# Keeping the upsampled rows out of x: logits per group and a second gather

## The chip, the cores and the metric

The kernel runs on one core of one Trainium2 chip. The metric is the device time of one launch in microseconds; the number shown for the kernel before is the median of three runs. The engines are TensorE (PE, with its weight loads PEld), VectorE (DVE), ScalarE (ACT), GpSimd (POOL) and SyncE (SP), whose queue issues most transfers.

## The reference

Two stages are computed: an attention with a downsampled and a local part, and a layer of eight experts over its result. Cut to what matters:

```python
def _attn_ref(q, k, v):                       # 8 batches, 8 heads, 576 tokens, 64 dims
    q_d, k_d, v_d = [z.reshape(B, H, 144, 4, D).mean(axis=3) for z in (q, k, v)]
    out_up = np.repeat(sm_attn(q_d, k_d, v_d), 4, axis=2)
    mask = np.abs(pos[:, None] - pos[None, :]) < 4
    out_local = masked softmax attention of q, k, v
    return out_up + out_local

def _moe_ref(x, w_gate, w1, w2):              # x: 4608 tokens x 512
    logits = x @ w_gate                       # 8 experts, 576 tokens each
    order = np.argsort(-logits.flatten())
    # in this order a token goes to an expert while the token is free and the expert has room
    for e in range(8):
        out[assigned == e] = np.maximum(x[assigned == e] @ w1[e], 0) @ w2[e]
```

`out_up` has one row for four tokens: 1152 different rows of 512 numbers, against 4608 rows of x. The logits are linear in x.

## The kernel before

**Attention** (class Attention) works on 36 units of 128 tokens, four and a half units to a batch. For each batch q, k and v are loaded and transposed, the downsampled attention is computed (`down`), and its rows are written from the tile `xu` to `up_dram` in DRAM (L387, L394). For each unit `loc_s`, `loc_t` and `loc_v` compute the local attention into the tile `x`. `load_up` (L416) loads the unit's 32 rows of `up_dram`, each into four partitions (256 KB). `log_a` (L484) adds them into x, on DVE for the first 28 units and on POOL after that. `store` (L487) writes x to `x_dram`. `log_t` transposes x on PE (L494) and writes it as two float16 parts with ACT (L498) and DVE (L499). `log_m` multiplies them by the gate weights (L509, L512) and sums into the logits `lg` (L514).

The order of this stage is written by hand. `run` gives each piece of work a time in units, `at`, sorts by it and issues the work in that order on every queue. The times of a unit's steps are its number plus the lags of this table:

```python
LOC = {'up': 1.7, 'st': 4.6, 't': 1.3, 'lm': 8.07, 's0': 0.33, 's1': 0.331, 'lt': 5.61, 'v0': 1.83, 'v1': 1.831, 'add': 4.5}
UPQ = STQ = "sync"
```

`end[b]` is the time at which the downsampled attention of batch b is done; no up load stands ahead of it. Loads of q, k and v, the stores and the loads of up rows all go through SP's queue, in this order.

**Routing** (class Routing) finds for each expert the tokens that it gets: DVE compares the logits' codes with thresholds (L703), PE counts (L733, L744), and the chain ends in the token numbers `idx` (L1004). `ro.phase` does it for one expert; that of the next expert runs beside the present one.

**Experts** (class Experts). `gather` fetches an expert's 576 rows of `x_dram` in five indirect transfers on POOL (L1068), of 128 rows each and of 64 the last. For experts 0 and 1 `piece` transposes each part on PE (L1077), with ACT and DVE writing the two float16 parts `xt` (L1080, L1081). For later experts ACT and DVE first write the parts as `xs` (L1087, L1088), and SP's queue transposes them by a transfer (L1089). `mlp` computes the hidden layer in eight slices f of 128 (L1104; for each slice 24 matmuls into `pH`, then ACT and DVE write `ht`, L1117 and L1120), then five chunks of output rows (L1133, `pX`), their eviction (L1139) and their scatter on POOL (L1142). The next expert's weights are split into float16 parts beside it (L1051 on ACT, L1053 on DVE). In expert 0 the table

```python
GET0 = {3: (0, 1), 4: (2, 3, 4)}
```

sets expert 1's pieces: 0 and 1 are transposed after the matmuls of chunk 3, ahead of chunk 4, the rest after chunk 4. From here on the framework's scheduler sets the order, by priorities and by when it takes operands to be ready.

Of the kernel before, what the change touches and what calls it, by code (L numbers as in the profile page):

```python
# [49 lines left out]
LOC = {'up': 1.7, 'st': 4.6, 't': 1.3, 'lm': 8.07, 's0': 0.33, 's1': 0.331, 'lt': 5.61, 'v0': 1.83, 'v1': 1.831, 'add': 4.5}  # L50
# [3 lines left out]
UPQ = STQ = "sync"  # L54
NSW = 2
UB = 3
XB = 6
# [3 lines left out]
ADDU = 28  # L61
DX = 0
SETUP = {25:0,35:26}
# [26 lines left out]
class Attention:  # L90
    def __init__(self, ctx, tc, q, k, v, wg, ident, identb, maskc, x_dram, up_dram, lg, big, more=()):
        self.tc, self.nc = tc, tc.nc
        self.q, self.k, self.v = q, k, v
        self.x_dram, self.up_dram, self.lg = x_dram, up_dram, lg
# [22 lines left out]
        self.vw, self.vd, self.qz, self.qdz, self.qdt, self.sw, self.ptw = [], [], [], [], [], [], []  # L117
        self.sd = cst.tile([128, 9, G], F32, name="sd")
# [291 lines left out]
    def load_up(self, u):  # L410
        for b in {4 * u // NW, (4 * u + 3) // NW}:
            for g in range(2):
                self.need(("v", b, g))
        t = self.wk.tile([128, HD], F32, name="up", bufs=UB)
        src = self.up_dram[32 * u:32 * u + 32]
        getattr(self.nc, UPQ).dma_start(t, bass.AP(tensor=src.tensor, offset=src.offset, ap=[[HD, 32], [0, 4], [1, HD]]))  # L416
        self.up[u] = t

# [59 lines left out]
    def log_a(self, u):  # L481
        nc = self.nc
        x = self.x[u]
        (nc.gpsimd if u >= ADDU else nc.vector).tensor_tensor(x, x, self.up[u], op=OP.add)  # L484

# [3 lines left out]
    def log_t(self, u):  # L489
        nc = self.nc  # L490
        x = self.x[u]
        p = self.ps.tile([128, 4, 128], F32, name="g", bufs=8)
        for c in range(4):
            nc.tensor.transpose(p[:, c], x[:, 128 * c:128 * c + 128], self.ident)  # L494
        xt = self.wk.tile([128, 2, 4, 128], F16, name="xt", bufs=TB)
# [4 lines left out]
                                                              op0=OP.mult, op1=OP.subtract), ("x", u))  # L500
        self.xt[u] = xt

    def log_m(self, u):
        nc = self.nc
        self.need(("x", u))
        xt = self.xt.pop(u)
# [7 lines left out]
        nc.vector.tensor_reduce(self.lg[:, u], l.rearrange("p s e -> p e s"), axis=AX.X, op=OP.add)  # L514
# [23 lines left out]
    def run(self, after, ready):  # L538
# [14 lines left out]
        for b in range(B):  # L553
# [27 lines left out]
            "up": lambda u: lambda: self.load_up(u),  # L581
            "st": lambda u: lambda: self.store(u),
            "add": lambda u: lambda: self.log_a(u),
# [5 lines left out]
        for u in range(NT):  # L589
            if u > 1:  # L590
                work.append((u - VWT, 0, 0, lambda u=u: self.load_vw(u), False))
            for j, (name, lag) in enumerate(LOC.items()):
                at = u + lag
                if lag >= 2.0:

                    at += max(E0 - u * E1, 0.0) - max(u - UE, 0) * CE * int(lag - 1)
                if name == "up":
                    at = max(at, end[(4 * u + 3) // NW])
                work.append((at, 2, j, stage[name](u), name in PEL))
                if name == "lm" and u in SETUP:  # L600
                    steps = after(SETUP[u], u + 1)
                    work += [(at + SPACE * k, 3, k, lambda g=steps: next(g, None), False) for k in range(24)]
# [405 lines left out]
class Experts:  # L1008
    def __init__(self, ctx, tc, x_dram, w1, w2, out, ident, ps, raw):
        self.tc, self.nc, self.x, self.w1, self.w2, self.out, self.ps = tc, tc.nc, x_dram, w1, w2, out, ps  # L1010
        self.raw = raw
# [47 lines left out]
    def gather(self, idx, first):  # L1059


        nc = self.nc
        xt = self.wk.tile([128, 2, 4, CAP], F16, name="xt")
        xgs = []
        for c, (s0, n) in enumerate(SL):
            xg = self.wk.tile([128, HD], F32, name="xg", bufs=5)
            with self.tc.high_priority():
                self.fetched = nc.gpsimd.indirect_dma_start(out=xg[:n], out_offset=None, in_=self.x,  # L1068
                                                            in_offset=bass.IndirectOffsetOnAxis(
                                                                ap=idx[:n, c:c + 1], axis=0))  # L1070
            xgs.append(xg)
# [22 lines left out]
    def mlp(self, w, xt, idx, in1, in2):  # L1094
# [4 lines left out]
        for f in range(8):  # L1099
            p = self.ps.tile([128, 2, 512], F32, name="pH", bufs=2)  # L1100
            seq = [(d, a, b) for d in range(4) for a, b in ((0, 0), (0, 1), (1, 0))]
            for s, (s0, s1) in enumerate(CUT):
                for j, (d, a, b) in enumerate(seq):
                    mm = nc.tensor.matmul(p[:, s, :s1 - s0], w[d][a][:, 128 * f:128 * f + 128], xt[:, b, d, s0:s1],  # L1104
                                          start=j == 0, stop=j == len(seq) - 1)
            if f == AFT:
                aft = mm
            with self.tc.high_priority():
                los = []
                for i, (n0, n1) in enumerate(((0, 256), (256, 320))):  # L1110
                    q = p[:, :, n0:n1] if i == 0 else p[:, 1:, n0:n1]
                    m = q.shape[1]
                    s0 = 0 if i == 0 else 512
                    hi = ht[:, f, s0:s0 + m * (n1 - n0)].rearrange("p (s n) -> p s n", s=m)
                    o0 = CAP + 64 if i == 0 else CAP
                    lo = ht[:, f, o0:o0 + m * (n1 - n0)].rearrange("p (s n) -> p s n", s=m)
# [4 lines left out]
            in1(f, last)  # L1121
# [27 lines left out]

FREE = 0  # L1150
# [8 lines left out]
def moe_attention(tc, q, k, v, wg, w1, w2, cst, out):  # L1159
    nc = tc.nc  # L1160
    with ExitStack() as top:
# [3 lines left out]
        up_dram = dr.tile([B * G, HD], F32, name="up_dram")  # L1165
        lg = keep.tile([128, NT, E], F32, name="lg")
# [121 lines left out]
```

## Time and profile before

| | us |
|---|---|
| median of three runs (798.14 to 803.59) | 799.38 |
| the profiled execution | 802.95 |
| its span on the core | 801.2 |
| PE busy | 684.2 (85%) |
| DVE busy | 563.2 (70%) |
| ACT busy | 331.7 (41%) |
| POOL busy | 249.4 (31%) |

The mean granted clock of TensorE is 0.929 of full speed. The numbers in the next sections come from this one execution. A line of its timeline gives start, length, engine, line of the kernel, operation, tiles and count, and in brackets how long the engine was idle before it and what ended that. The attention ends at about 299 us, when the last logits are reduced; the routing of the first expert takes until 327 us, when its first gather starts; the experts take the rest.

### The profile page before, as it was taken

The numbers are of one execution on the slowest core, as the hardware profiler recorded it, in microseconds if no ns is written. First come the engines' busy times: TensorE is split into PE (matmuls) and PEld (weight loads), VectorE is DVE, ScalarE is ACT, GpSimd is POOL, SyncE is SP. The second block draws the span as 40 slices with busy tenths as digits, with TensorE's granted clock in tenths as the row PEclk, the third lists the DMA queues.
The fourth block names the chain that finished last, engine by engine and source line by source line (L and its number), as shares of the span: only waits on it lengthen the run. The fifth ranks groups of instructions, "written<-read, shape, count | busy, mean of one in ns | idle before, by whom it ended". The sixth has DMA issues, their size and how long they took to land. (4 is left out here: it accounts for less than half of the span.)

```text
span 801.2 us, 21182 instructions
## 1 busy us (share of the span) xinstructions
PE 684.2 (85%) x8565; PEld 470.8 (59%) x8565; DVE 563.2 (70%) x1679; ACT 331.7 (41%) x631; POOL 249.4 (31%) x274
## 2 busy tenths in 40 slices
PE   6587978895998863499899899999989979999994
PEld 4576867774787752365465365475456456574752
DVE  7787977986797887787969779798859536172210
ACT  3266766672766440341525225244224224252210
POOL 8273463735356340300700302131420500401001
PEclk9599998997989995599999999999989989999998
DMA  9939989797999750712506625471932942704001
GB/s 255 217 107 241 234 216 271 191 269 191 235 236 214 185 179 1 232 39 97 209 24 225 144 90 201 99 256 40 245 140 72 308 118 101 178 2 98 20 27 34
DMA packets 148133, 125.00 MB, mean 156 GB/s; under 512 B 92228, under 2 KB 122436, under 8 KB 148036
## 3 DMA queue, kind: packets, MB, share of 16 engines
q1 hardware_dynamic: 140656, 102.12, 48.1%
q0 software_dynamic: 6432, 20.98, 8.3%
q8 instruction: 68, 1.11, 0.6%
q10 hardware_dynamic: 948, 0.55, 0.3%
q14 instruction: 29, 0.24, 0.1%
HBM read 95.30 MB, written 21.23 MB: 145 GB/s over the span
## 5 line engine op out<-in xcount | busy, mean ns | idle before, releaser
L1104 PE MATMUL pH<-xt,wh 128*128 128x256 f16 (+1 forms) x1024 | 201.6, 292 | 6.1 <-DMA xt<-xs 5.3
L1133 PE MATMUL pX<-wh,ht 128*128 128x512 f16 (+1 forms) x640 | 182.9, 386 | 1.9 <-DVE xt L1081 1.9
L1142 POOL DMA_INDIRECT out_dram<-y,idx x40 | 50.1, 1253 | 317.1 <-ACT y L1139 262.4
L1104 PE MATMUL pH<-xt,wl 128*128 128x320 f16 (+1 forms) x512 | 148.7, 291 | 0.0
L1133 PEld LDWEIGHTS <-ht 128*128 128x128 f16 (+1 forms) x960 | 83.0, 101 | 91.2 <-issue 8.4
L1133 PE MATMUL pX<-wl,ht 128*128 128x512 f16 (+1 forms) x320 | 120.2, 386 | 0.0
L1104 PEld LDWEIGHTS <-wh 128*128 128x128 f16 x1024 | 98.9, 99 | 33.8 <-issue 9.0
L1117 ACT ACTIVATE ht<-pH 128x512 f16<-128x512 f32 (+1 forms) x128 | 45.5, 407 | 135.5 <-PE pH L1104 135.5
L1053 DVE SCALAR_TENSOR_TENSOR wl<-nat,wh 128x512 f16<-128x512 f32 x128 | 84.8, 683 | 3.1 <-ACT wh L1051 0.6
L1120 DVE SCALAR_TENSOR_TENSOR ht<-pH,ht 128x512 f16<-128x512 f32 (+1 forms) x128 | 52.6, 451 | 43.2 <-ACT ht L1117 42.7
L1139 ACT ACTIVATE y<-pX 128x512 f32<-128x512 f32 (+1 forms) x40 | 23.8, 594 | 136.5 <-PE pX L1133 86.2
L1068 POOL DMA_INDIRECT xg<-x_dram,idx x40 | 48.2, 1204 | 81.9 <-DVE idx L1004 32.7
L1051 ACT ACTIVATE wh<-nat 128x1024 f16<-128x1024 f32 x64 | 66.6, 1056 | 10.2 <-DMA nat<-in_moe_w_dram 10.0
L292 PE MATMUL g<-ident,nat 128*128 128x128 f32 x256 | 41.6, 291 | 20.3 <-DMA nat<-in_q_dram 15.9
L1104 PEld LDWEIGHTS <-wl 128*128 128x128 f16 x512 | 50.8, 99 | 12.7
L465 ACT COPY pt<-g 64x512 f32<-64x512 f32 x72 | 41.8, 581 | 34.8 <-PE g L454 33.6
L476 PE MATMUL g<-vw,pt 128*64 128x65 f32 x1152 | 44.4, 229 | 3.3 <-ACT pt L465 3.0
L476 PEld LDWEIGHTS g<-vw,pt 128*64 128x64 f32 x1152 | 39.4, 142 | 9.4 <-ACT pt L465 5.9
L278 ACT COPY kt<-g 64x512 f32<-64x512 f32 (+1 forms) x56 | 35.1, 626 | 23.4 <-PE g L292 15.6
L292 PEld LDWEIGHTS g<-ident,nat 128*128 128x128 f32 x256 | 30.5, 148 | 23.5 <-issue 17.5
L278 ACT COPY qz<-g 64x512 f32<-64x512 f32 (+1 forms) x52 | 32.9, 633 | 23.4 <-PE g L292 22.3
L265 POOL TENSOR_TENSOR gtmp<-qz 64x576 f32<-64x576 f32 x28 | 32.4, 1157 | 32.0 <-DVE kdt L268 30.3
(219 smaller groups left out, 1167.4 us busy)
## 6 DMA issues: line engine op xcount, KB each, us to landing
nat<-in_moe_w_dram SPq DMA_DIRECT2D x28, 1024.0 KB
vw<-in_v_dram SPq DMA_DIRECT2D x136, 96.0 KB
up<-up_dram SPq DMA_DIRECT2D x36, 256.0 KB
x_dram<-x SPq DMA_DIRECT2D x36, 256.0 KB
nat<-in_q_dram SPq DMA_DIRECT2D x16, 512.0 KB
nat<-in_k_dram SPq DMA_DIRECT2D x16, 512.0 KB
nat<-in_v_dram SPq DMA_DIRECT2D x14, 512.0 KB
up_dram<-xu SPq DMA_DIRECT2D x16, 128.0 KB
```

The lines of the kernel that those rows point to most:

```text
L278: self.nc.scalar.copy(out, in_)
L292: nc.tensor.transpose(p[:, a, :, fp], src[:, 4 * hh + 2 * a + s, 2 * fp:2 * fp + 2].rearrange("p f d -> p (f d)"), self.ident)
L465: self.nc.scalar.copy(out, in_)
L476: nc.tensor.matmul(o[64 * i:64 * i + 64, 65 * h:65 * h + 65], pt[:, 2 * g + i, h].rearrange("p b q -> p (b q)"), self.vw[u % 4][:, i, 4 * ...
L1051: nc.scalar.activation(hi, r, AF.Copy, scale=sc)
L1053: nc.vector.scalar_tensor_tensor(lo[:, a:a + LOP], r[:, a:a + LOP], sc, hi[:, a:a + LOP], op0=OP.mult, op1=OP.subtract)
L1068: self.fetched = nc.gpsimd.indirect_dma_start(out=xg[:n], out_offset=None, in_=self.x, in_offset=bass.IndirectOffsetOnAxis(ap=idx[:n, c:c ...
L1104: mm = nc.tensor.matmul(p[:, s, :s1 - s0], w[d][a][:, 128 * f:128 * f + 128], xt[:, b, d, s0:s1], start=j == 0, stop=j == len(seq) - 1)
L1117: last = nc.scalar.activation(hi, q, AF.Relu)
L1120: nc.vector.scalar_tensor_tensor(lo, q, 0.0, hi, op0=OP.max, op1=OP.subtract)
L1133: mm = nc.tensor.matmul(p[o:o + m], ht[:, f, h0:h0 + m], w[4 + f // 2][b][:, 512 * (f % 2):512 * (f % 2) + 512], start=j < parts, stop=j > ...
L1142: i = nc.gpsimd.indirect_dma_start(out=self.out, in_=y[:n], in_offset=None, out_offset=bass.IndirectOffsetOnAxis(ap=idx[:n, c:c + 1], axis=0))
```

## The change

x is stored and multiplied by the gate without the up rows: the loads of each unit's up rows and the adds are gone, and the lags of store and logits are smaller. Instead each of nine groups of 128 up rows (four units' worth) is loaded once, transposed and multiplied by the gate like a unit (`up_t`, `up_m`); its logits go to a small DRAM tile (`up_put`), come back with each row in four partitions (`up_get`), and are added to the logits (`up_add`, on POOL, the last on DVE). In the experts the token's row of `up_dram` is number `idx >> 2`; a second indirect transfer with an add on the way puts it on each gathered row of x. The first expert's hidden layer is computed for tokens 0 to 255 of all slices and then for tokens 256 to 575.

```diff
-LOC = {'up': 1.7, 'st': 4.6, 't': 1.3, 'lm': 8.07, ..., 'lt': 5.61, 'v0': 1.83, 'v1': 1.831, 'add': 4.5}
+LOC = {'st': 2.6, 't': 1.3, 'lm': 5.46, ..., 'lt': 3.0, 'v0': 1.83, 'v1': 1.831}
+UP = (("load", 0.35), ("t", 1.0), ("m", 1.9), ("put", 2.4), ("get", 3.1), ("add", 3.7))
+UPL = (("load", 0.2), ("t", 0.8), ("m", 1.3), ("put", 1.6), ("get", 2.1), ("add", 2.6))
-UB = 3
-XB = 6
+UB = 2
+XB = 4
-SETUP = {25:0,35:26}
+SETUP = {27: 0, 35: 28}
+SETLAG = 0.35
...
-    def load_up(self, u):
...
-        src = self.up_dram[32 * u:32 * u + 32]
-        getattr(self.nc, UPQ).dma_start(t, bass.AP(tensor=src.tensor, offset=src.offset, ap=[[HD, 32], [0, 4], [1, HD]]))
+    def up_load(self, j):
+        for g in range(2):
+            self.need(("v", (128 * j + 127) // G, g))
+        t = self.wk.tile([128, HD], F32, name="up", bufs=UB)
+        self.nc.sync.dma_start(t, self.up_dram[128 * j:128 * j + 128])
+        self.up[j] = t
+    def up_t(self, j):
+        self.logits_t(self.up[j], ("up", j), "xtu", 1)
+    def up_m(self, j):
+        self.up[j] = self.wk.tile([128, E], F32, name="lup")
+        self.logits_m(self.up[j], ("up", j))
+    def up_put(self, j):
+        d = self.lup_dram[j]
+        self.nc.sync.dma_start(bass.AP(tensor=d.tensor, offset=d.offset, ap=[[E, 4], [4 * E, 32], [1, E]]), self.up[j])
+    def up_get(self, j):
+        d = self.lup_dram[j]
+        self.nc.sync.dma_start(self.lgu[:, 4 * j:4 * j + 4].rearrange("p u e -> p (u e)"),
+                               bass.AP(tensor=d.tensor, offset=d.offset, ap=[[4 * E, 32], [0, 4], [1, 4 * E]]))
+    def up_add(self, j):
+        a, b = [t[:, 4 * j:4 * j + 4].rearrange("p u e -> p (u e)") for t in (self.lg, self.lgu)]
+        (self.nc.vector if j == 8 else self.nc.gpsimd).tensor_tensor(a, a, b, op=OP.add)
...
-    def log_a(self, u):
-        nc = self.nc
-        x = self.x[u]
-        (nc.gpsimd if u >= ADDU else nc.vector).tensor_tensor(x, x, self.up[u], op=OP.add)
...
+            if u % 4 == 3:
+                j = u // 4
+                for name, lag in UPL if j == 8 else UP:
+                    at = end[(128 * j + 127) // G] + lag
+                    if name == "add":
+                        at = max(at, lmt + 0.1)
+                    work.append((at, 2, 100 + j, lambda f=getattr(self, "up_" + name), j=j: f(j), name in "tm"))
...
+        up = self.wk.tile([128, 5], I32, name="upx")
+        with self.tc.high_priority():
+            for r, a, b in ((128, 0, 4), (64, 4, 5)):
+                nc.vector.tensor_scalar(up[:r, a:b], idx[:r, a:b], 2, None, op0=OP.arith_shift_right)
...
+        for c, more in ROWORDER:
+            n = SL[c][1]
             with self.tc.high_priority():
+                self.fetched = nc.gpsimd.indirect_dma_start(
+                    out=xgs[c][:n], out_offset=None, in_=self.up if more else self.x,
+                    in_offset=bass.IndirectOffsetOnAxis(ap=(up if more else idx)[:n, c:c + 1], axis=0),
+                    **({"compute_op": OP.add} if more else {}))
...
+        if first:
+            for s, (s0, s1) in enumerate(CUT):
+                for f in range(8):
...
+                    aft = product(p[:, h, :s1 - s0], f, s0, s1)
+                    last = evict(f, [(p[:, h:h + 1, :256], s0, 256)] + ([(p[:, h:h + 1, 256:320], 512, 64)] if s else []))
+                    if s:
+                        in1(f, last)
...
+ROWORDER = ((0, 0), (1, 0), (0, 1), (1, 1), (2, 0), (3, 0), (4, 0), (2, 1), (3, 1), (4, 1))
```

`logits_t` and `logits_m` are the bodies of `log_t` and `log_m`, now used for both. `product` and `evict` are the old body of a slice; the other experts run it as before. `in1` issues the splits of the weights, so that those of expert 0's second weights stand in its second half. These weights are loaded on POOL after `self.fetched`, which is now the last gather of up rows.

SP's queue where one batch ends. Before, the load of up rows stands between the write of `xu` and the next batch's q and k (`natt`, `nat`):

```order
L487 DMA x_dram<-x 128x512
L387 DMA up_dram<-xu 128x256 x2
L394 DMA up_dram<-xu 8x16x64
L416 DMA up<-up_dram 128x1x512
L200 DMA natt<-in_q_dram 64x1x256 x2
L200 DMA natt<-in_k_dram 64x1x256 x2
L215 DMA nat<-in_q_dram 128x4x256
L215 DMA nat<-in_k_dram 128x4x256
```

The same place after:

```order
L390 DMA up_dram<-xu 128x256 x2
L397 DMA up_dram<-xu 8x16x64
L203 DMA natt<-in_q_dram 64x1x256 x2
L203 DMA natt<-in_k_dram 64x1x256 x2
L218 DMA nat<-in_q_dram 128x4x256
L218 DMA nat<-in_k_dram 128x4x256
L232 DMA vw_130<-in_v_dram 48x8x64
L232 DMA vw_130<-in_v_dram 32x8x64
L232 DMA vw_130<-in_v_dram 6x8x64
L232 DMA vw_130<-in_v_dram 48x8x64 x2
L417 DMA up<-up_dram 128x512
```

The q and k loads and a unit's v loads have moved ahead of the load that needs `xu` in DRAM. Later in the same batch the queue has the new pair, with loads of v (`vw`) and stores around it:

```order
L500 DMA x_dram<-x 128x512
L232 DMA vw_132<-in_v_dram 48x8x64 x4
L429 DMA lup_dram<-lup 4x32x8
L500 DMA x_dram<-x 128x512
L433 DMA lgu<-lup_dram 128x1x32
L232 DMA vw_129<-in_v_dram 48x8x64 x4
L500 DMA x_dram<-x 128x512
```

The get (L433) reads what the put (L429) wrote, two places ahead of it. POOL's queue where the experts begin, before:

```order
L484 TENSOR_TENSOR x<-x,up 128x512 x6
L1068 DMA xg<-x_dram,idx 128x512 x4
L1068 DMA xg<-x_dram,idx 64x512
L1023 TENSOR_LOAD ei
L1023 ISA x2
L1035 ISA
L1035 DMA nat<-in_moe_w_dram 128x4x512
```

and after:

```order
L438 TENSOR_TENSOR lg<-lg,lgu 128x32
L1098 DMA xg<-x_dram,idx 128x512 x4
L1098 DMA xg<-x_dram,idx 64x512
L1098 DMA xg<-up_dram,upx 128x512 x4
L1098 DMA xg<-up_dram,upx 64x512
L1047 TENSOR_LOAD ei
L1047 ISA x2
L1059 ISA
L1059 DMA nat<-in_moe_w_dram 128x4x512
```

Whatever the table ROWORDER lists, all gathers of x stand first and all gathers of up rows behind them. DVE while expert 0's rows come in, before (`xt` are the pieces, `cmp` the compares of expert 1's routing):

```order
L1081 SCALAR_TENSOR_TENSOR xt<-pX,xt 128x4x128 x2
L824 TENSOR_TENSOR s<-s,m 128x36
L825 TENSOR_TENSOR eq<-eq,codes 128x288
L1081 SCALAR_TENSOR_TENSOR xt<-pX,xt 128x4x64
L829 TENSOR_SCALAR h<-s 128x36
```

and after:

```order
L726 TENSOR_TENSOR cmp_6039<-xh,first 128x1280
L726 TENSOR_TENSOR cmp_6039<-xh,first 128x1024
L726 TENSOR_TENSOR cmp_6134<-xl,first 128x1280
L1111 SCALAR_TENSOR_TENSOR xt<-pX,xt 128x4x128
L764 TENSOR_SCALAR cs<-pR 128x16
L726 TENSOR_TENSOR cmp_6134<-xl,first 128x1024
```

Before, the compares come after all five pieces; now three of four come ahead of the first piece.

More of the change, by code (lines that the diff above doesn't have):

```diff
@@ L53 @@
 GW = 2
-UPQ = STQ = "sync"
+STQ = "sync"
 NSW = 2
-UB = 3
-XB = 6
+UB = 2
+XB = 4
 NPT = 2
@@ L90, with __init__ @@
 class Attention:
-    def __init__(self, ctx, tc, q, k, v, wg, ident, identb, maskc, x_dram, up_dram, lg, big, more=()):
+    def __init__(self, ctx, tc, q, k, v, wg, ident, identb, maskc, x_dram, up_dram, lup_dram, lg, big, more=()):
         self.tc, self.nc = tc, tc.nc
         self.q, self.k, self.v = q, k, v
-        self.x_dram, self.up_dram, self.lg = x_dram, up_dram, lg
+        self.x_dram, self.up_dram, self.lup_dram, self.lg = x_dram, up_dram, lup_dram, lg
         nc = self.nc
@@ L513, in log_m @@
                              skip_group_check=True)
-        nc.vector.tensor_reduce(self.lg[:, u], l.rearrange("p s e -> p e s"), axis=AX.X, op=OP.add)
+        nc.vector.tensor_reduce(out, l.rearrange("p s e -> p e s"), axis=AX.X, op=OP.add)
     def transposes(self, b):
@@ L601, in run @@
                     steps = after(SETUP[u], u + 1)
-                    work += [(at + SPACE * k, 3, k, lambda g=steps: next(g, None), False) for k in range(24)]
+                    work += [(at + SETLAG + SPACE * k, 3, k, lambda g=steps: next(g, None), False) for k in range(24)]
+                if name == "lm":
+                    lmt = at
+            if u % 4 == 3:
[5 more added lines that the diff above has]
+                    work.append((at, 2, 100 + j, lambda f=getattr(self, "up_" + name), j=j: f(j), name in "tm"))
         work.sort(key=lambda z: z[:3])
@@ L1008, with __init__ @@
 class Experts:
-    def __init__(self, ctx, tc, x_dram, w1, w2, out, ident, ps, raw):
+    def __init__(self, ctx, tc, x_dram, up_dram, w1, w2, out, ident, ps, raw):
         self.tc, self.nc, self.x, self.w1, self.w2, self.out, self.ps = tc, tc.nc, x_dram, w1, w2, out, ps
+        self.up = up_dram
         self.raw = raw
@@ L1092, in gather, with mlp @@
         return xt, piece if first else piece_dma
-    def mlp(self, w, xt, idx, in1, in2):
+    def mlp(self, w, xt, idx, in1, in2, first=False):
         nc = self.nc
@@ L1177, in moe_attention @@
             ro.open(ctx, ps, ident)
-            ex = Experts(ctx, tc, x_dram, w1, w2, out, ident, ps, big)
+            ex = Experts(ctx, tc, x_dram, up_dram, w1, w2, out, ident, ps, big)
             with tc.high_priority(TOP):
@@ L1223, in in2 @@
                                     split(2 * c + 1)
-                ex.mlp(w, xt, idx, in1, in2)
+                ex.mlp(w, xt, idx, in1, in2, i == 0)
                 if i == 0:
```

77 lines of the change are left out of this document (38 added, 39 removed).

## The prediction

> **What bounds the kernel now.** I read the windows first (stretch, length, busy time of PE, weight loads, DVE, ACT and POOL with instruction counts, TensorE clock, DMA share, GB/s), then the DMA view of the attention stretch, the timeline at the batch boundaries, and the timeline where experts 0 and 1 begin.
>
> ```profile
> 60.00:260.00 200.00, 166.12 (x3720) 143.05 (x3718) 160.03 (x413) 126.34 (x246) 95.00 (x121) 0.93 0.93 230
> ...
> 340.00:390.00 50.00, 49.40 (x396) 29.08 (x395) 41.04 (x144) 19.03 (x36) 6.48 (x5) 1.00 0.33 121
> 400.00:801.00 401.00, 373.60 (x2815) 223.22 (x2812) 242.89 (x781) 128.63 (x244) 76.67 (x67) 0.97 0.42 121
> 186.00:188.00 2.00, 0.98 (x12) 0.77 (x8) 1.97 (x4) 1.06 (x2) 1.92 (x2) 1.00 0.01 3
> ...
> 200.00:220.00 20.00, 18.33 (x388) 15.96 (x386) 15.71 (x41) 15.02 (x30) 6.33 (x9) 1.00 1.01 240
> ```
>
> The steady attention stretch (60 to 260 us, 26 of the 36 units) is held by transfers: the DMA share is 0.93, and 1.01 in the slice 200–220, with PE close behind at 0.83 and 0.92. The experts are held by PE: 373.60 of 401 us, DMA at 0.42. So what leaves DMA in attention counts; in the experts only what makes PE wait counts. What the attention stretch transfers:
>
> ```profile
> GB/s 287 245 263 176 135 257 278 262 272 254 239 102 256 287 258 283 234 102 147 281 348 216 272 233 196 84 237 242 308 270 233 148 142 252 302 237 276 228 252 99
> DMA packets 70844, 45.98 MB, mean 230 GB/s; under 512 B 43075, under 2 KB 64067, under 8 KB 70803
> ...
> q1 hardware_dynamic: 70803, 45.40, 91.4%
> ...
> up<-up_dram SPq DMA_DIRECT2D x26, 256.0 KB
> ```
>
> The second limit is the DMA queue at each batch boundary. Its load of the up rows waits there until the rows just written have landed, and the next batch's q and k stand behind it (SP queue, then PE, then the SP waits as total, times, longest):
>
> ```profile
> 113.42 0.65 SPq L394 DMA_DIRECT2D up_dram<-xu  x1
> 115.97 0.53 SPq L416 DMA_DIRECT2D up<-up_dram  x1
> ...
> 181.99 0.65 SPq L394 DMA_DIRECT2D up_dram<-xu  x1
> 186.73 0.53 SPq L416 DMA_DIRECT2D up<-up_dram  x1
> ...
> 123.97 1.09 PE L292 MATMUL g<-ident,nat 128*128 128x128 f32 x4 [5.22 <-DMA nat<-in_q_dram]
> ...
> 194.56 0.66 PE L292 MATMUL g<-ident,nat 128*128 128x128 f32 x2 [7.58 <-DMA nat<-in_q_dram]
> ...
> SPq L416 <- DMA up_dram<-xu: 15.2, 8, 4.0
> ```
>
> SP stands from 114.07 to 115.97 (1.90 us) and from 182.64 to 186.73 (4.09 us), 15.2 us in eight waits. DMA runs dry (0.01 in 186–188), and PE later waits 5.22 and 7.58 us for q.
>
> **Attention, part by part.** *Transfers removed and added.* Of 36 up loads 26 lie in the stretch. One moves 0.262 MB: 1.06 us at the queue's mean (45.40 MB in 91.4% of 200 us), 0.75 us at the best slice, 348 GB/s. I take 0.75, since its rows are 2 KB and most packets that make the mean are under 512 B: 26 × 0.75 = 19.5 us off. Added are 6.5 of nine group loads of the same 0.262 MB (4.9 us) and 6.5 pairs of put and get in pieces of 32 and 128 B. A pair costs 0.13 us by its 32 KB and 0.66 us by 256 packets of the queue's 2.58 ns; between these 0.3, so 2 us. Net −12.6 us of DMA time; bounds −10 and −20.
>
> *The boundary.* q and k now come 0.55 us of load issue plus 1.9 to 4.1 us of wait earlier, at about four boundaries. Part of it is the same DMA time as above; the share of 0.93 leaves 14 us empty, and I take a third, −4.5. What is late next is the up load itself, which nobody needs before its group's logits, and a new wait: the get stands in SP's queue until its put has landed, with v loads and x stores behind it. The eight waits on xu are nearest: 1.9 us each, but in mid batch, where loads stand queued ahead of what PE needs.
>
> *Engines.*
>
> ```profile
> L484 DVE TENSOR_TENSOR x<-x,up 128x512 f32<-128x512 f32 x27 | 28.7, 1064 | 8.1 <-DMA up<-up_dram 8.1
> ...
> L494 PE MATMUL g<-ident,x 128*128 128x128 f32 x104 | 17.7, 295 | 0.0
> ...
> L499 DVE SCALAR_TENSOR_TENSOR xt<-g,xt 128x512 f16<-128x512 f32 x25 | 17.1, 683 | 0.7 <-ACT xt L498 0.7
> ...
> L509 PE MATMUL g<-wg,xt 128*128 128x16 f16 x96 | 6.1, 172 | 0.1
> L512 PE MATMUL g<-wg,xt 128*128 128x8 f16 x96 | 5.8, 166 | 0.0
> ```
>
> Smaller edits first: the nine POOL adds of 32 columns replace eight of 512 columns; the setup of the routing moves two units later beside the same work; fewer buffers for x (4) and up rows (2) stand against a store two units earlier and a row that is no longer held by an add. I cost them at nothing: POOL is busy 95 of 200 us, and the six x tiles covered a store that came two units later.
>
> DVE loses 28.7 us of adds and gains 6.5 × 0.85 us (one eviction of 683 ns, one reduce); it was off the path, so this is worth nothing by itself. PE gains for each group what a unit's logits cost: 17.7/26 + 6.1/24 + 5.8/24 = 1.2 us, 7.6 us in all. That makes 173.7 us of PE in a stretch where 0.92 is the most seen: 189 us, or 182 at the full clock that a stretch without dry spells would have (166 us at 0.93). So PE allows −11 to −18, DMA −17. I take −17; bounds −8 (the new wait takes back what the old gave) and −25. The 10 units outside the stretch share its pattern at a lower DMA share: −3.
>
> *The end of attention.*
>
> ```profile
> 280.02 0.64 SPq L394 DMA_DIRECT2D up_dram<-xu  x1
> 281.71 0.54 SPq L416 DMA_DIRECT2D up<-up_dram  x1
> ...
> 298.91 0.17 DVE L514 TENSOR_REDUCE lg<-g 128x8 f32<-128x16 f32 x1
> ```
>
> From the last load at 281.71 the new chain (landing, logits, put, get, add) takes about 15 us, an estimate of three landings of 2 to 3 us and 1.2 + 0.6 + 0.68 + 0.17 us of work besides its queueing; it ends near 296.4, before the last unit's own reduce at 298.91. Cost 0; −1 to +3. Attention: −20.
>
> **Expert 0.** All five up gathers stand behind the five x gathers on POOL (see the order above), so the product by halves starts no sooner than the whole one did.
>
> ```profile
> 326.99 1.52 POOL L1068 DMA_INDIRECT xg<-x_dram,idx  x1 [32.31 <-DMA nat<-in_moe_w_dram]
> 328.81 1.48 POOL L1068 DMA_INDIRECT xg<-x_dram,idx  x1 [0.30 <-issue]
> ...
> 330.91 1.11 PE L1077 MATMUL pX<-ident,xg 128*128 128x128 f32 x4 [6.11 <-DMA xg<-x_dram,idx]
> ...
> 333.64 0.92 POOL L1068 DMA_INDIRECT xg<-x_dram,idx  x1 [0.30 <-issue]
> ...
> 339.15 0.69 PE L1077 MATMUL pX<-ident,xg 64*128 64x64 f32 x4
> ```
>
> A gather issues in 0.92 to 1.52 us plus 0.30, and lands 2.40 us after (328.51 to 330.91). Five more take 333.64 + 0.92 − 326.99 + 0.30 = 7.87 us. Before, the last piece was transposed at 339.15, 2.2 us after it landed (336.96), beside early products; so the gain of overlap is 2.2 at most and the cost 5.7 to 7.9. I take +7. The eight added evictions on ACT and DVE lie beside PE, which is busy 49.40 of 50 us in 340–390 where DVE has 9 us free; w2's splits, now in the second half only, may press there (up to +3). Upper end 11.
>
> **Expert 1.**
>
> ```profile
> 385.04 1.39 POOL L1068 DMA_INDIRECT xg<-x_dram,idx  x1 [2.14 <-issue]
> ...
> 390.22 0.60 PE L1077 MATMUL pX<-ident,xg 128*128 128x128 f32 x4
> 390.53 1.41 DVE L703 TENSOR_TENSOR cmp<-xh,first 128x1280 bf16<-128x1280 int16 x2
> 390.54 4.16 POOL L1068 DMA_INDIRECT xg<-x_dram,idx  x1 [0.30 <-PE pX L1133]
> ...
> 394.53 0.57 PE L1133 MATMUL pX<-wh,ht 128*64 128x512 f16 x1 [1.87 <-DVE xt L1081]
> 395.00 1.47 POOL L1068 DMA_INDIRECT xg<-x_dram,idx  x1 [0.30 <-issue]
> 396.77 2.79 POOL L1142 DMA_INDIRECT out_dram<-y,idx  x1 [0.30 <-issue]
> 398.93 0.66 PE L1077 MATMUL pX<-ident,xg 128*128 128x128 f32 x4
> ```
>
> PE has the transposes of pieces 0 and 1 ahead of expert 0's last chunk. Its first up gather starts where the scatter stands, 396.77, and lands at 396.77 + 1.5 + 2.4 = 400.7; the second at 402.5. Then come the transposes (0.66) and the last chunk (394.53 to 398.93, 4.4 us): 407.6 against 398.93, so +8.7; PE idles from 392 and restarts at a lower clock: +9. If the held gather (4.16 us, beside the compares) were quick, 2.7 less, +6; 13 with one more held. The scatters behind the gathers wait 8 us, and nobody waits for them. Expert 0's second weights, issued on POOL behind its last gather, come 8 us later, and so does their first split, now in the second half.
>
> **Later experts** fetch an expert ahead; the row nearest to trouble is expert 5's first product:
>
> ```profile
> 648.33 0.69 PE L1104 MATMUL pH<-xt,wh 128*128 128x320 f16 x2 [5.26 <-DMA xt<-xs]
> ```
>
> Once PE already waits for transposed rows. The up gathers add 1.2 MB an expert to transfers at 0.42: +1.5, from −1 to +6 (this wait doubled).
>
> **The sum**, against the profiled 802.95 us (span 801.2): −20 + 0 + 7 + 9 + 1.5 = −2.5, so 800.5. That execution lies 3.6 above the median of 799.4, so 797 for the median.
>
> **The rivals.**
> *Faster.* The boundary's dry time goes wholly and the gathers cost their low ends: −25 − 5 + 5.7 + 6 + 0.5 = −18, 782. For it: PE's waits for q of 5.22 and 7.58 us. Against: PE's 173.7 us.
> *Slower: compares hold the gathers.* In expert 0 the first compares now stand on DVE beside the up gathers. The row at 390.54 took 4.16 us beside compares from 390.53, its neighbours 1.39 and 1.47: +2.7 each. Five of ten held give +13.5, 810; from four on it decides (+10.8, past 1%). Against: only one of expert 1's five was held.
> *The gathers are never held*, and 390.54 was slow for another cause: 2.7 less in expert 1, 794. The row speaks against it, one time. The Trainium skill, page "SBUF — State Buffer", section "Who interferes with whom", says that a tensor_tensor with both inputs in SBUF contends with GpSimd's reads only and infers that descriptor generation needs the write interface, so compares would delay no gather. By that rule the sum is 794 and the slower case falls away; the 4.16 us beside the compare says otherwise.
> *The new wait takes the old one's place.* If each get stops SP for 1.9 to 4.1 us with loads missing behind it, 6.5 of them give back 12 us or more; attention falls to −8 − 2 and the sum is +7.5, 807. For it: v loads stand behind the get. Against: SP is ahead of PE there in mid batch.
>
> **How the numbers follow.** A measurement of this kernel tells about 1% (8 us) from no change. The forecast and the case of gathers never held lie within it: 0.36 and 0.06, together 0.42; their own range is 791 to 805. Faster 0.35 (776 to 791). Slower 0.14 by held gathers and 0.09 by the new wait, 0.23 (807 to 822). 780 to 813 leaves about a tenth out at each side.
>
> **What would show it.** In the profile after: SP's wait on xu gone from ahead of q, PE's waits for q under 3 us, the DMA share of the stretch near 0.93 over some 183 us; the last reduce near 280 us; PE's dense product of expert 0 seven us later after its first gather; a wait of about 8 us at expert 1's first transposes; POOL rows over 2.5 us beside compares if gathers are held. An attention end later than 290, or earlier than 272, breaks the sum, and so does an expert 1 that starts without a gap.

## The result, and the profile after

The changed kernel took 892.0 us (median of 4 runs, 887.4 to 899.0) where the kernel before took 801.5 (4 runs, 798.1 to 806.2): a ratio of 1.113, 95% interval 1.103 to 1.123. The forecast was 797 and its range ended at 813.

The two profiled executions (spans 801.2 and 889.2 us) are laid side by side in the table, by the starts of the last write of the logits, of the first gather, and of the last or first matmul of an expert's hidden layer.

| stretch | before | after | difference | forecast |
|---|---|---|---|---|
| start to last logits | 298.9 | 350.8 | +51.9 | −20 |
| last logits to first gather | 28.1 | 29.8 | +1.7 | 0 |
| first gather to the end of expert 0's hidden layer | 40.8 | 60.0 | +19.2 | +7 |
| from there to expert 1's first product | 31.6 | 39.4 | +7.8 | +9 |
| from there to the end | 401.8 | 409.1 | +7.3 | +1.5 |

Of the 88 us, 52 are lost in the attention, where the forecast had a gain, and 34 in the experts, where it had 17.5. The windows of the changed kernel, in the columns of the prediction:

```profile
60.00:260.00 200.00, 139.94 (x3011) 124.20 (x3011) 118.36 (x328) 104.51 (x204) 75.19 (x105) 0.83 0.68 168
...
340.00:400.00 60.00, 18.78 (x340) 15.28 (x338) 41.60 (x159) 12.68 (x22) 16.90 (x11) 0.59 0.32 86
```

In 60 to 260 us DMA went from a share of 0.93 to 0.68, as the removal of loads would have it. But PE, too, does less: 139.94 us busy in place of 166.12, 3011 matmuls in place of 3720. No engine is near its full time there, so something is waited for. PE's waits up to the end of the attention (engine, line, tile waited for, us in all, times, longest):

```profile
PE g L512 <- DMA up<-up_dram: 62.3, 9, 11.7
...
PE g L295 <- DMA nat<-in_q_dram: 0.6, 1, 0.6
```

Of the wait for q, 15.9 us before, 0.6 is left, and nine waits for the new group loads have come, 62.3 us in all. One of them, in the timeline of SP and then PE:

```profile
125.38 0.62 SPq L397 DMA_DIRECT2D up_dram<-xu  x1
126.05 1.22 SPq L203 DMA_DIRECT2D natt<-in_q_dram  x2
127.32 1.22 SPq L203 DMA_DIRECT2D natt<-in_k_dram  x2
128.59 1.36 SPq L218 DMA_DIRECT2D nat<-in_q_dram  x1
129.99 0.51 SPq L218 DMA_DIRECT2D nat<-in_k_dram  x1
...
132.92 0.68 SPq L417 DMA_DIRECT2D up<-up_dram  x1
...
138.27 1.09 PE L512 MATMUL g<-ident,up 128*128 128x128 f32 x4 [9.68 <-DMA up<-up_dram]
```

The load of up rows (L417) is issued 6.9 us after the write's last transfer, behind the q, k and v loads, and it lands 5.3 us later, with their data ahead of it. PE has had its transposes next in its own order since 128.6 and stands for 9.68 us.

At expert 0 the gathers are issued on POOL, beside DVE's splits of the first weights (L1077), and PE waits for up rows:

```profile
380.61 5.77 POOL L1098 DMA_INDIRECT xg<-x_dram,idx  x1 [34.64 <-DVE used L981]
...
391.76 1.59 POOL L1098 DMA_INDIRECT xg<-up_dram,upx  x1 [0.30 <-DVE cmp L726]
393.66 1.55 POOL L1098 DMA_INDIRECT xg<-up_dram,upx  x1 [0.30 <-issue]
...
396.55 1.12 PE L1107 MATMUL pX<-ident,xg 128*128 128x128 f32 x4 [18.14 <-DMA xg<-up_dram,upx]
...
397.35 1.53 POOL L1098 DMA_INDIRECT xg<-up_dram,upx  x1 [0.31 <-issue]
...
402.63 1.97 PE L1107 MATMUL pX<-ident,xg 128*128 128x128 f32 x8 [4.50 <-DMA xg<-up_dram,upx]
```

The first gather takes 5.77 us instead of 1.52. The first up gather ends at 393.35 and PE starts on its rows 3.2 us later, where the prediction had 2.40. For the next piece PE waits much longer, and the trace's semaphores say for what: its first instruction at 402.63 waits for the fourth up gather, the one at 397.35, and that one had itself waited for the second gather of x. So the framework put the up gathers into the order of pieces 0, 2, 3, 1, 4. The fourth ends at 398.88, and PE starts 3.75 us later. The first half of the hidden layer, tokens 0 to 255, needs pieces 0 and 1, and so could not start before four of the five up gathers had been issued.

### The profile page after: what moved, and what is told of

It is laid out like the page before. It is cut to its first block, busy times and chain, and to the rows that moved or that the text cites. A ratio compares the mean times of both kernels' runs of the same rounds, so it can differ in the third digit from the quotient of the medians.

```text
span 889.2 us, 21454 instructions
## 1 busy us (share of the span) xinstructions
PE 702.5 (79%) x8673; PEld 488.4 (55%) x8673; DVE 549.9 (62%) x1694; ACT 338.7 (38%) x648; POOL 303.3 (34%) x314
## 4 chain that ended last, share of the span: by engine, by line
PE 48%; DVE 13%; DMA 13%; issue 11%; SPq 5%; ACT 5%; POOL 3%; another core or an unknown queue 0%; POOLq 0%; ACTq 0%; DVEq 0%
PE pH L1133 14%; PE pX L1180 11%; DMA up<-up_dram 5%; PE g L494 3%; PE g L512 3%; DMA xg<-up_dram,upx 3%; POOL xg L1098 3%; PE g L454 2%; SPq L232 2%; PE pR L756 2%; PE g L295 2%; PE g L376 2%; PE g L472 2%; DMA nat<-in_moe_w_dram 1%; DVE cmp L726 1%
## 5 line engine op out<-in xcount | busy, mean ns | idle before, releaser
L1133 PE MATMUL pH<-xt,wh 128*128 128x320 f16 (+1 forms) x1024 | 201.1, 291 | 7.5 <-DMA xt<-xs 4.0
L1180 PE MATMUL pX<-wh,ht 128*128 128x512 f16 (+1 forms) x640 | 185.6, 390 | 0.0
L1145 ACT ACTIVATE ht<-pH 128x64 f16<-128x64 f32 (+2 forms) x136 | 46.9, 393 | 139.0 <-PE pH L1133 135.1
L1077 DVE SCALAR_TENSOR_TENSOR wl<-nat,wh 128x512 f16<-128x512 f32 x128 | 85.0, 683 | 8.2 <-ACT wh L1075 6.1
L1148 DVE SCALAR_TENSOR_TENSOR ht<-pH,ht 128x64 f16<-128x64 f32 (+2 forms) x136 | 53.9, 434 | 44.5 <-ACT ht L1145 43.9
L1098 POOL DMA_INDIRECT xg<-x_dram,idx x40 | 52.1, 1301 | 82.9 <-DVE used L981 34.6
L1098 POOL DMA_INDIRECT xg<-up_dram,upx x40 | 64.3, 1607 | 35.6 <-DMA xg<-x_dram,idx 19.5
L512 PE MATMUL g<-ident,up 128*128 128x128 f32 x36 | 9.3, 410 | 62.3 <-DMA up<-up_dram 62.3
L494 PE MATMUL g<-vw,pt 128*64 128x65 f32 x1152 | 45.2, 232 | 12.3 <-ACT pt L483 9.4
L268 POOL TENSOR_TENSOR gtmp<-kt 128x576 f32<-128x576 f32 x7 | 8.0, 1146 | 122.4 <-ACT kt L281 53.1
L1118 DVE SCALAR_TENSOR_TENSOR xs<-xg,xs 128x512 f16<-128x512 f32 (+1 forms) x30 | 19.8, 685 | 41.5 <-ACT xs L1117 41.4
```

The lines of the kernel that those rows point to most:

```text
L494: nc.tensor.matmul(o[64 * i:64 * i + 64, 65 * h:65 * h + 65], pt[:, 2 * g + i, h].rearrange("p b q -> p (b q)"), self.vw[u % 4][:, i, 4 * ...
L1077: nc.vector.scalar_tensor_tensor(lo[:, a:a + LOP], r[:, a:a + LOP], sc, hi[:, a:a + LOP], op0=OP.mult, op1=OP.subtract)
L1098: self.fetched = nc.gpsimd.indirect_dma_start(out=xgs[c][:n], out_offset=None, in_=self.up if more else self.x, in_offset=bass.IndirectOff ...
L1133: mm = nc.tensor.matmul(p, w[d][a][:, 128 * f:128 * f + 128], xt[:, b, d, s0:s1], start=j == 0, stop=j == len(seq) - 1)
L1145: last = nc.scalar.activation(hi, q, AF.Relu)
L1148: nc.vector.scalar_tensor_tensor(lo, q, 0.0, hi, op0=OP.max, op1=OP.subtract)
```

## The experiments

The runs were taken on three chips, each beside runs of the kernel before on the same chip (medians 794 to 800 us); ratios are compared across chips. The last logits of the attention of before were written at 293.6, 297.8, 298.9 and 301.8 us in four kernels that have it unchanged, so differences under about 8 us in that number say nothing by themselves. The stretch from expert 1's first product to the end scatters more: 401.8 to 405.7 us in the three traces with the experts of before, 404.8 to 419.1 in the eight with adding gathers.

**The steps of the groups later.**

```diff
+UPW = (("load", 0.35), ("t", 2.4), ("m", 3.1), ("put", 3.6), ("get", 4.15), ("add", 4.6))
-                for name, lag in UPL if j == 8 else UP:
+                for name, lag in UPL if j == 8 else UP if j == 7 else UPW:
```

> The changed kernel, with the transposes, products, put, get and add of the groups of up rows 0 to 6 moved 1.2 to 1.4 units later behind their load (groups 7 and 8 as they were). Theory A: PE stands in its fixed order at the up rows' transposes (62.3 us of waits for up in nine places), because their load is now late behind the next batch's loads; then seven of these waits (about 54 us) go, the waits of groups 0 to 6 come under 2 us each, and the time falls by 40 to 54 us, to 838 to 852. Rival B: the wait is only where a shortage of transfers shows (the loads of q, k, v arrive late in any case); then PE waits as long for other tiles and the time stays within 15 us of 892.

855.2 us, ratio 1.072 (1.065 to 1.080): by the ratios 33 us less than the changed kernel. The waits for up fall from 62.3 to 17.9, and the last logits come at 303.6 instead of 350.8. Theory A holds in its mechanism; the gain is a little smaller than it gave, and three of the waits of groups 0 to 6 are still over 2 us (up to 3.8). The move leaves something out: the add of group 6 now comes behind the routing's first reduce over the logits of its units (277.08 against 271.23), so their up rows do not reach the routing. The run shows the waits and is no finished mend.

**The load first.** The other way to the same end: the load goes back ahead of q and k.

```diff
-UP = (("load", 0.35), ("t", 1.0), ("m", 1.9), ("put", 2.4), ("get", 3.1), ("add", 3.7))
+UP = (("load", 0.0), ("t", 1.0), ("m", 1.9), ("put", 2.4), ("get", 3.1), ("add", 3.7))
```

> The changed kernel with the load of up rows moved back to where the kernel before has it, right behind the write of xu and ahead of the next batch's q and k; all else as changed. Theory A (PE waits only because the load is late behind q, k and v): the load is issued 2 to 4 us sooner and lands in 2 to 3 us instead of 5, so each of eight waits shrinks from 4 to 12 us to some 3 to 5, while SP waits for xu again and q comes later; the time falls by 15 to 40 us, to 852 to 877. Rival B (the stretch is short of transfers in any case): within 10 of 892.

840.5 us, ratio 1.056 (1.049 to 1.063), more than expected. For groups 1 to 5 PE starts on the rows 2.7 to 3.5 us after the load's issue, where the changed kernel took 5.1 to 5.8. The waits for up are 14.4 us in six places, those for q 1.6, and the last logits come at 303.9. One number of 0.35 in a table of lags costs some 46 us (1.113 − 1.056 of 801).

**Both mends.**

```diff
-UP = (("load", 0.35), ("t", 1.0), ("m", 1.9), ("put", 2.4), ("get", 3.1), ("add", 3.7))
+UP = (("load", 0.0), ("t", 1.0), ("m", 1.9), ("put", 2.4), ("get", 3.1), ("add", 3.7))
+UPW = (("load", 0.0), ("t", 1.9), ("m", 2.6), ("put", 3.2), ("get", 3.8), ("add", 4.3))
-                for name, lag in UPL if j == 8 else UP:
+                for name, lag in UPL if j == 8 else UP if j == 7 else UPW:
```

> The changed kernel with both mends of the late load: the load of up rows right behind the write of xu, and the steps of groups 0 to 6 0.6 to 0.9 units later. Theory A: PE's waits for up of groups 0 to 6 fall under 1 us each, the attention ends at 290 to 298, and the time is 830 to 840. Rival B (what PE no longer waits for up it then waits for q and k, or for the get's place in SP's queue): it ends after 300, as with either mend alone (304).

842.5 us, ratio 1.051 (1.045 to 1.058), just above what was expected and not clear of the run before it. One wait for up of 5.4 us is left, that of group 7, whose steps were not moved, and the last logits come at 297.4: the waits of groups 0 to 6 are gone, and the attention is where it was before the change, not ahead of it. Here, too, group 6's add comes behind the routing's first reduce (267.23 against 264.07), and its up rows are left out of the routing.

**No groups.** The upper end of what the removals can bring: the steps of the groups are left out, so the logits are those of the local part alone.

```diff
-            if u % 4 == 3:
+            if u < 0:
```

> The changed kernel with the removals of the attention alone: no group of up rows is loaded, transposed, multiplied, put, got or added, so that the up rows are left out of the logits (they stay in the experts' input). Theory A (all of the attention's loss is in the groups' steps): the attention ends before 290 us, where the changed kernel's ended at 351, and the time is 824 to 832. By the prediction's own terms for transfers and boundary it would end near 272. If it ends at 285 to 292 instead, PE and the chain of each unit, not the transfers, hold the stretch once 10% of them is gone.

825.4 us, ratio 1.031 (1.025 to 1.037), as expected; the end of the attention, 282.3, lies between the 272 of the prediction's terms and the 285 to 292 of the other case. The window of the stretch, and the last logits of this run and of the run with both mends:

```profile
60.00:260.00 200.00, 176.07 (x4014) 155.24 (x4012) 152.47 (x426) 135.08 (x266) 92.52 (x126) 0.95 0.83 200
```

```profile
282.29 0.17 DVE L532 TENSOR_REDUCE lg<-g 128x8 f32<-128x16 f32 x1
```

```profile
297.41 0.19 DVE L439 TENSOR_TENSOR lg<-lg,lgu 128x32 f32<-128x32 f32 x1
```

With the loads and adds gone and nothing put in their place DMA falls to 0.83, PE rises to 0.88, and the attention ends 16.6 us sooner, not the 27 that the prediction's terms for the removed loads, the boundary and the rest add up to (19.5, 4.5 and 3). The groups, even where nobody waits much for them, then cost 15 us (297.4 against 282.3). The matmuls of the nine groups (10.5 us busy in the run with both mends; 11 by the prediction's 1.2 each) and the 5.4 us wait would account for it; that was not taken apart further.

**The boundary alone.** The kernel before with its own up load behind the next q and k:

```diff
-                    at = max(at, end[(4 * u + 3) // NW])
+                    at = max(at, end[(4 * u + 3) // NW] + 0.35)
```

> The kernel before with one number changed: the up load of a batch's first units stands 0.35 units later, behind the next batch's first q and k loads, as in the changed kernel; the adds stay where they were. The prediction's step on the boundary: SP's wait on xu goes from ahead of q and k, PE's waits for q (5 to 8 us) shrink to under 3 us, and the time falls by 4 to 12 us, to 789 to 797. Rival: the queue's dry time only moves (q and k arrive no sooner, or the up rows come late for their adds), 798 to 806.

793.4 us, ratio 0.9915 (0.989 to 0.994): somewhat faster than the kernel before, and clear of its noise, as expected. Its window, then PE's wait for q in the same stretch in the kernel before, which has no row left here:

```profile
60.00:260.00 200.00, 172.51 (x3926) 147.75 (x3921) 168.95 (x440) 132.59 (x261) 100.25 (x127) 0.97 1.00 243
```

```profile
PE g L292 <- DMA nat<-in_q_dram: 12.8, 2, 7.6
```

DMA's dry time is gone (share 1.00, 243 GB/s in place of 230). The same move that cost 46 us in the changed kernel gains 7 here. What differs is the reader. DVE came to the adds that need these rows 2.6 us or more after the load's issue and stood 6.8 us in the whole stretch (8.1 before), where PE, in the changed kernel, came to the transposes of groups 1 to 5 2.4 to 5.9 us ahead of the load's issue and stood 7.9 to 11.7 us at each.

**The boundary, further.**

```diff
-                    at = max(at, end[(4 * u + 3) // NW])
+                    at = max(at, end[(4 * u + 3) // NW] + 0.8)
```

> The kernel before with the up load 0.8 units behind the end of its batch's downsampled attention (0.35 gave a ratio of 0.9915). If the transfers' dry time was all that was lost, it is gone already: within 3 us of the 0.35 run. If the adds come to wait for the later load: 3 to 8 us slower than that.

799.5 us, ratio 0.998 (0.994 to 1.001): the gain is gone. DVE's waits for up rows in 60 to 260, at 0.8 and at 0.35:

```profile
DVE x L484 <- DMA up<-up_dram: 13.8, 5, 5.1
```

```profile
DVE x L484 <- DMA up<-up_dram: 6.8, 4, 2.6
```

They have doubled, with DMA back at 0.97, as the second of the two expectations has it; that these 7 us are the whole of the lost gain was not shown.

**Experts alone.** The attention of before with the experts of the changed kernel.

> The attention of the kernel before with the experts of the changed one; x holds the up rows already, so that they are counted twice in the experts' input. Theory A (attention and experts lose apart from each other): 801 plus 30 to 40, 831 to 841. Rival D (the experts lose mostly because the attention ends late, with its last transfers beside them): under 820.

835.9 us, ratio 1.0485 (1.040 to 1.057). As expected, the experts' loss stands by itself, some 37 us, and does not need the late attention.

**No second gathers.**

```diff
-ROWORDER = ((0, 0), (1, 0), (0, 1), (1, 1), (2, 0), (3, 0), (4, 0), (2, 1), (3, 1), (4, 1))
+ROWORDER = ((0, 0), (1, 0), (2, 0), (3, 0), (4, 0))
```

> The changed kernel without the second gathers: the up rows are left out of the experts' input. Theory A: the two gathers per piece, one waiting behind the other, cost the experts about 35 of the 90 us (13 us at expert 0, 18 at expert 1 in the trace); without them 892 falls to 855 to 862. Rival C: the product by halves, and the weights loaded behind, cost most of it; then it falls by less than 15 us.

856.9 us, ratio 1.0725 (1.067 to 1.078), as expected: 33 to 35 us of the loss go with the second gathers, and with the loads of the second weights, which no longer stand behind them. The halves are still in it, and from the first gather to the end of expert 0's hidden layer it takes 43.3 us, against 40.8 before and 60.0 as changed.

**The second gathers without the add.** From the kernel with only the experts changed:

```diff
-                    in_offset=bass.IndirectOffsetOnAxis(ap=(up if more else idx)[:n, c:c + 1], axis=0),
-                    **({"compute_op": OP.add} if more else {}))
+                    in_offset=bass.IndirectOffsetOnAxis(ap=(up if more else idx)[:n, c:c + 1], axis=0))
```

> As the run with only the experts changed (835.9 us), with the second gathers as plain copies: they overwrite the gathered rows of x, so the experts see the up rows alone and the local part is left out. Count, places and waits of the gathers stay. Theory E (an adding gather lands late, 3 to 7 us after it was issued against 2.4, since it moves its bytes at half the rate): the pieces of experts 0 and 1 come sooner and the time falls by 8 to 20 us, to 816 to 828. Rival F (the number of gathers on POOL and the wait for x's landing cost it, not the add): 831 to 838.

808.6 us, ratio 1.0165 (1.010 to 1.023), against 1.0485 with the add: without the add 26 us of the experts' 37 are gone, more than expected. By the traces 6.7 of them lie before the end of expert 0's hidden layer, 2.4 from there to expert 1's first product, and 23 behind it (414.8 us from there to the end with the add, 391.4 without). The last part is not the add alone: 391.4 is less than the 401.8 of the kernel before, and another kernel with plain gathers, below, takes 412.0 there. The page's rows of the 40 second gathers with the add (the run of the experts alone) and without it:

```profile
L1075 POOL DMA_INDIRECT xg<-up_dram,upx x40 | 64.0, 1600 | 31.8 <-DMA xg<-x_dram,idx 18.3
```

```profile
L1075 POOL DMA_INDIRECT xg<-up_dram,upx x40 | 39.7, 992 | 31.2 <-DMA xg<-x_dram,idx 18.0
```

They are issued in 1.6 us instead of 0.99. Their transfers differ more. With the add, the timeline and the window (length, engines, clock, DMA share, GB/s) of expert 0's second gathers:

```profile
329.58 1.59 POOL L1075 DMA_INDIRECT xg<-up_dram,upx  x1 [0.31 <-DVE am L831]
331.47 1.85 POOL L1075 DMA_INDIRECT xg<-up_dram,upx  x1 [0.30 <-issue]
...
334.29 1.12 PE L1084 MATMUL pX<-ident,xg 128*128 128x128 f32 x4 [14.76 <-DMA xg<-up_dram,upx]
...
335.47 1.54 POOL L1075 DMA_INDIRECT xg<-up_dram,upx  x1 [0.30 <-issue]
...
341.12 1.97 PE L1084 MATMUL pX<-ident,xg 128*128 128x128 f32 x8 [5.24 <-DMA xg<-up_dram,upx]
...
329.60:341.20 11.60, 1.67 (x23) 1.52 (x24) 4.08 (x10) 2.02 (x5) 9.62 (x7) 0.50 0.78 127
```

and without it:

```profile
333.19 0.95 POOL L1075 DMA_INDIRECT xg<-up_dram,upx  x1 [0.30 <-DVE h L829]
...
336.52 1.11 PE L1083 MATMUL pX<-ident,xg 128*128 128x128 f32 x4 [12.83 <-DMA xg<-up_dram,upx]
...
337.28 0.94 POOL L1075 DMA_INDIRECT xg<-up_dram,upx  x1 [0.30 <-issue]
...
333.20:340.50 7.30, 1.58 (x22) 1.42 (x22) 4.87 (x12) 2.02 (x5) 6.08 (x7) 0.50 0.57 190
```

The plain gather ends at 334.14 and PE starts on its rows 2.38 us later, the prediction's 2.40. The adding one takes 3.1 us. For its next piece PE waits, in both runs, for the fourth up gather: 4.1 us after that gather's end with the add (335.47 + 1.54 to 341.12), 2.3 without it (337.28 + 0.94 to 340.50). With the add the transfers move 127 GB/s at a share of 0.78, plain ones 190 at 0.57: 163 against 333 GB/s for a full share, half the rate.

**Whole slices instead of halves**, once as changed and once with plain gathers:

```diff
-                ex.mlp(w, xt, idx, in1, in2, i == 0)
+                ex.mlp(w, xt, idx, in1, in2)
```

> The changed kernel with the first expert's product in whole slices, as before. Theory A (the second gathers carry the experts' loss, the halves nothing): within 5 of 892. Rival C (the splits of the second weights, packed into the second half, hold the product): 5 to 15 us less.

> As the run with plain second gathers (808.6 us; the up rows overwrite the gathered x, the local part is left out), with the first expert's product in whole slices. The prediction's term for expert 0 (five more gathers on POOL at plain price, +7) then stands alone: from the first gather to the last product of expert 0's hidden layer 47 to 49 us, where the kernel before took 40.8 and the plain gathers with halves 52.2; the time falls by 3 to 6 us. Rival: the halves cost nothing here, since the plain gathers land early: 52 us.

As changed: 880.8 us, ratio 1.107 (1.100 to 1.114), about 5 us less, on the border of the two theories, and the intervals overlap. In the trace the hidden layer of expert 0 takes 31.3 us instead of 35.9. Where the halves lose it, in the changed kernel:

```profile
430.00:435.00 5.00, 2.64 (x20) 1.92 (x21) 4.90 (x27) 1.64 (x4) 0.00 (x0) 1.00 0.00 0
```

```profile
432.36 0.45 PE L1133 MATMUL pH<-xt,wh 128*128 128x320 f16 x2 [3.00 <-DVE ht L1148]
```

DVE is full there (4.90 of 5 us) with evictions, the second weights' splits and the routing of expert 1, and PE waits 3.0 us for an eviction. With plain gathers expert 0 came out close to what was expected (47 to 49), 49.3 us from the first gather to the end of the hidden layer against 52.2, but the time did not: 825.7 us, ratio 1.031 (1.024 to 1.037), worse than the 1.0165 with halves. The trace has it far away, in experts 3 to 5, where PE waits for the routing's counts:

```profile
PE pR L744 <- DVE cs L741: 9.2, 5, 4.1
```

There is no such wait in the run with halves. The edit does not touch these experts, and their instructions stand in the same order on every engine in both traces, but for a few at the edges. From expert 1's first product to the end this run takes 412.0 us and the one with halves 391.4. Of these 20.6 us 9.2 are the waits above, and PE's granted clock in experts 4 and 5 is 0.95 and 0.94 where it was 1.00 and 0.97; why the counts come late here stays open.

**Two tiny writes among the splits.**

```diff
                 with tc.issue_after(ro.done.ins):
+                    for k in range(2):
+                        nc.vector.memset(ex.wk.tile([128, 8], F32, name="pause", bufs=1), 0.0)
                     for k in range(4):
                         split(k)
```

> The changed kernel with two tiny writes (128x8) put on DVE among the splits of the first weights, which run beside the first gather. Theory G (the first gather took 5.77 us because the splits held it, and whether they do hangs on where in them it starts): it falls to about 1.5 us, the time by some 4 us. Rival H (the splits have no part in it; the first gather pays for something else): 5.77 us again.

```profile
374.95 0.07 DVE L1236 MEMSET pause<- 128x8 f32 x1
375.07 0.68 DVE L1077 SCALAR_TENSOR_TENSOR wl<-nat,wh 128x512 f16<-128x512 f32 x1
375.27 1.55 POOL L1098 DMA_INDIRECT xg<-x_dram,idx  x1 [33.73 <-DVE n L976]
```

The first gather takes 1.55 us. In the seven traces that have the changed attention, without the pause, it takes 5.77 to 5.86; in the six with the attention of before 1.51 or 1.52. So the splits hold it or not by where in them it starts: the run of six splits that follow each other begins 1.00 to 1.09 us after the gather's start in the seven, and the gather then ends 1.1 us after the last of them; in the pause run and the six it begins 1.12 to 1.18 us after it. The one time taken, 879.5 us, has no partner to weigh 4 us against; from the first gather to the end of expert 0's hidden layer only 1.1 us were gained (58.9), and two other kernels with a held gather and halves took 62.1 and 62.6 there, so 1.1 us is within the scatter.

## Why the prediction was wrong

The step that failed first is in the part on the boundary: "What is late next is the up load itself, which nobody needs before its group's logits". The group's logits are exactly what needed it, 0.65 units behind, and their transposes stand in PE's fixed order. The order printed ahead of the prediction shows the load behind the next batch's transfers of q, k and v; the table of lags shows the transposes 0.65 units (some 5 us) after it, and PE, which runs ahead of SP's queue there, came to them before the load was even issued. I put the two beside each other for SP and not for PE. That is 62 us of waits, and moving the steps or the load each takes most of them away (1.113 to 1.072 and 1.056, both to 1.051). The new wait that I did price, the get behind its put, was not it: SP stands 12.3 us for it over the whole kernel, and PE's waits for q, k and v stay under 10 us.

```profile
SPq L433 <- DMA lup_dram<-lup: 12.3, 8, 2.0
```

Step by step:

- *Transfers removed, −12.6, and the boundary, −4.5, with −3 outside the stretch:* the direction was right and the sizes shared out wrongly. The boundary alone gives some −7 (ratio 0.9915), and its last logits come at 286.9; boundary and removal together bring them to 282.3, −16.6. So the removal behind a mended boundary is worth some 5 to 10 us, with a scatter of the same size. That PE (0.88 of the stretch) and the chain of each unit are the next limit fits this and was not tried. Two figures of the working do not come out, and the forecast does not hang on them: a pair of put and get is 20 KB by its shapes, not 32, and 173.7 us of PE at the full clock would be 176 (173.7 × 0.93 / 0.92), not 182.
- *Groups' work on PE, 1.2 us each:* about right, 10.5 us measured for nine. With one wait left the groups cost 15 us. Against the removal they leave nothing: with both mends the attention ends at 297.4 against 298.9.
- *End of attention, 0:* right as far as the chain of put and get goes; the last get is issued at 343.49, 7 us ahead of the last unit's own reduce. What makes the end late are the waits for the loads, 4.2, 4.3 and 1.8 us of the 62.3 for the last three groups.
- *Expert 0, +7, at most 11; measured +19.2.* Whole slices with plain gathers took 49.3 us against 40.8, so the term as it was worked out, five more gathers at 2.40 us to landing, is +8.5. The halves add 2.9 (52.2; beside adding gathers 4.7, 60.0 against 55.3), the add on the way 6.7 (58.9); the last 1.1 (60.0), with the held first gather, is within the scatter. The failed step is the price of the up gathers: I took the plain gathers' rows for them, though no row before showed a gather with an add, and left no bound above for a transfer at half the rate.
- *Expert 1, +9; measured +7.8.* The wait came where it was forecast, 9.0 us at the first transposes against about 8, but the size is near by luck. With plain gathers the stretch takes 36.3 us, +4.7, so 2 to 3 us of it are the add here too, which the term did not have, and the number of gathers was priced too high by about 4:

```profile
471.72 1.09 PE L1107 MATMUL pX<-ident,xg 128*128 128x128 f32 x4 [9.00 <-DMA xg<-up_dram,upx]
```

- *Later experts, +1.5; measured +7.3.* The stretches from expert 1's first product to expert 2's and from there to expert 3's are 6.3 and 5.7 us longer than before; the last ones are shorter and make up for part of it. ACT has to write the parts of expert 2 as soon as the rows land, and stands for them in its own order; DVE's compares come later by it, and PE waits 7.9 us for these where it waited 0.9 before. How much of the 7.3 is this and how much the scatter of the stretch is not shown. In the changed kernel:

```profile
534.94 0.63 ACT L1117 ACTIVATE xs<-xg 128x512 f16<-128x512 f32 x1 [10.26 <-DMA xg<-up_dram,upx]
```

- *The rival of held gathers* named the compares of expert 1's routing. Beside those the gathers of expert 0 took 0.95 to 1.80 us, and of expert 1's ten one took 3.60 beside compares, as one of five took 4.16 before; what was new was the first gather, held by the weights' splits. The Trainium skill, page "SBUF — State Buffer", section "Who interferes with whom", says that a DVE instruction with two SBUF inputs contends with GpSimd instructions that read SBUF; the splits are of that kind, and the 5.77 us that two tiny writes turn into 1.55 agrees, though gathers that start in the middle of the same splits take only 0.94 to 1.49. Its inference, made for tensor_tensor, that descriptor generation would be spared does not fit the 3.60 and 4.16 us beside the compares.

That attention and experts each lose by themselves is shown by the runs that change one of them. Why the adding gather moves its bytes at half the rate was not tried.

## What to carry to other kernels

A load that is moved back in a queue is hidden only if the first instruction that reads it, on every engine with a fixed order, comes late enough: here one and the same move gained 7 us where DVE came to its adds after the load's issue, and cost 46 where PE came to its transposes ahead of it. Price a transfer that computes on the way by a run of its own and not by the plain one; look up in the trace which of several transfers an engine really waits for, since a scheduler may have put them into another order; and where a transfer share falls together with the busy time of the next engine, look for a new wait before crediting the gain.

## What the runs showed of the hardware

An indirect gather with an add into SBUF moved its bytes at 163 GB/s for a full DMA share against 333 for the plain one, took 1.6 us to issue against 0.99, and the first and fourth of a row of five had landed 3.1 and 4.1 us after the end of their issue against 2.4 and 2.3. A POOL gather that started 1.00 to 1.09 us ahead of six back-to-back DVE splits took 5.77 to 5.86 us, one that started 1.12 to 1.18 us ahead of them 1.51 to 1.55, and those that started in the middle of them 0.94 to 1.49.
